# Attention and a gated feed-forward on one core: another order for pairs 0 to 17, and fp32 products of zeros ahead of the first transposes

## The chip, the core and the metric

The kernel runs on one core of a Trainium2 chip. The metric is device time in microseconds (us) for one execution; the time before is the median of three, 401.28 us (401.22 to 402.11). PE is the matrix engine (PEld its weight loads), DVE is VectorE, ACT is ScalarE, POOL is GpSimd, and SP is the engine whose queue issues most transfers.

## The reference

Cosine attention over 8 batches of 12 heads, 448 positions, 64 columns each, and behind it a feed-forward with a hard-swish gate:

```
q_n = q / (norm(q) + 1e-6);  k_n = k / (norm(k) + 1e-6)
scores = q_n @ k_n.T / tau;  attn = softmax(scores);  x = attn @ v
h = x @ w_in;  g = h * clip(h + 3, 0, 6) / 6;  out = g @ w_out
```

x has 3584 rows (8 x 448) of 768 columns, w_in is 768 x 2048, w_out 2048 x 768. All inputs and the output are fp32; the kernel multiplies in bf16.

## The kernel before, in words

Heads are worked on in pairs. There are 48 pairs (six to a batch). The first 18 pairs are run by a list written out by hand, PLAN (lines 21 to 63), one token for each step; from pair 18 (FIRST) on a loop (lines 1017 to 1073) does the same steps in a fixed order. A token only says in which order a step's instructions stand on the engines that it uses; every engine executes its own instructions in order, and waits on the other engines where data or a buffer requires it. So two tokens that use different engines may stand either way round without a difference, and two on one engine may not.

Items are the loads of q and k: items 2d and 2d + 1 are q and k (or the other way round from item 14 on) of pairs 2d and 2d + 1. The tokens that the change touches most, with the first number the item or the pair:

- LQ.j loads item j (line 201, SP queue) into one of seven buffers, which LQ.j can only reuse when the item seven before it has been normalised. LV.d loads v for two pairs, four issues on SP (line 216). W is the next piece of the weights (line 926), issued on POOL.
- SQ.j.e.c.n squares n of the seven column groups (128 columns each) of item j, from group c on, on engine e: a is ACT (line 227), p is POOL, v is DVE (line 229). BN and BS get the sums of squares of some groups from moments on DVE (lines 250 to 256), RE reduces the squares to sums on DVE (line 244).
- NO.d.x makes the inverse norm r of one item or both: logarithm and exponential on ACT (lines 280, 281), and again logarithm and exponential on ACT (286, 287) or, with v, a reduction and a reciprocal on DVE (283, 284).
- NM.j.e multiplies an item by its r (line 297), whole or, with a last 0 or 1, one head pair's half of it. TR.j transposes it on PE (line 343, seven products with the identity), CQ and CK copy the transposed queries and keys out of PSUM (lines 363, 365), and CS the rest of the keys.
- SC.i.g makes the scores of pair i in four groups g on PE (lines 443, 446), EX.i.g their exponentials on ACT (line 464, 896 columns, or 448), VC casts v, VA.i.g multiplies the exponentials with v into PV on PE (line 486), FI divides by the sums on DVE (506, 507), BK transposes back on PE (line 520) and CX copies that to xT.
- U is the next unit of the feed-forward (six products of 448 columns, line 596, or eight of 384 columns, line 756), UH a piece of such a unit, UA and UV its ends on ACT (line 613) and DVE (line 619).
- DP.n and D.n are n products of zeros on PE (lines 938, 933), whose output is never read: 97 in all, 49 of them ahead of TR.1.

The scores of pairs 0 to 5 use two banks of PSUM (SC.i.g.bank). OPEN, behind EX.5.3, gives those back, and from pair 6 on scores, transposes and feed-forward units take turns on a ring of six banks. In the list before, a transpose can name its bank (Y or Z).

Of the kernel before, what the change touches and what calls it, by code (L numbers as in the profile page):

```python
# [66 lines left out]
def kernel(
# [209 lines left out]
    def inverse(tiles, pairs, on_vector):
        n2, le, r = tiles
        ln, nr = n2, pairs[:, :, :, 0]
        nc.scalar.activation(out=ln, in_=n2, func=AF.Ln)  # L280
        nc.scalar.activation(out=nr, in_=ln, func=AF.Exp, scale=0.5)
        if on_vector:
            nc.vector.tensor_reduce(out=le, in_=pairs, axis=AX.X, op=ALU.add)
            nc.vector.reciprocal(out=r, in_=le)
        else:
            nc.scalar.activation(out=le, in_=nr, func=AF.Ln, bias=eps_bias)
            nc.scalar.activation(out=r, in_=le, func=AF.Exp, scale=-1.0)  # L287

    def normalise(j, e, *heads):
# [7 lines left out]
        engines[e].tensor_tensor(  # L297
            out=nrm[:, :, g, :].rearrange("p c g d -> p g c d"),
            in0=raw_of[j][:, g, :, :],
            in1=n2_and_r[2][:, d % 2, j % 2, :]  # L300
            .rearrange("p (g c) -> p g c", g=2)[:, g, :]
            .to_broadcast([128, n, 7, D]),
# [631 lines left out]

    def busy_pv(n):
        first = ("VA", 0, 0) not in issued
        for _ in range(n):
            nc.tensor.matmul(  # L938
                PV[:, 0, 260:508], zeros[:, 0:128], zeros[:, 0:248], start=first, stop=first, skip_group_check=True
            )  # L940

# [174 lines left out]
```

## Time and profile before

| | us |
|---|---|
| median of three runs | 401.28 |
| the profiled execution, its time | 400.82 |
| its span, first to last instruction | 398.9 |
| first products of the feed-forward (line 596) start | 40.28 |
| first products of the second layer (line 756) start | 93.49 |

The profile is of one execution. A line of a timeline gives start, length, engine, source line, operation, output and input, shape and count, and in brackets how long the engine sat idle before it and what ended that. A chain of waits is followed back from the last instruction, at each step to what released it. Windows give the busy time of each engine in a stretch. A matmul's length has its latency in it, so products that follow each other overlap in the table, and a full PE need not be at its peak.

### The profile page before, as it was taken

What the parts mean: (1) busy time and instruction counts of PE and PEld (TensorE: products, weight loads), DVE (VectorE), ACT (ScalarE), POOL (GpSimd) and SP (SyncE); (2) the same over time, 40 slices, a digit from 0 to 9 for tenths busy, and PEclk for the clock granted to TensorE, in tenths of its full rate; (3) what the DMA queues carried; (4) which work ended last, traced back from release to release, by engine and by line L of the source; (5) the groups of instructions that cost most, each with busy time, mean ns of one, the idle gap of its engine ahead of it and who ended that gap; (6) DMA issues with size and microseconds to landing.
All of it is one profiled execution on the core that took longest, in us unless ns stands there. A gap on an engine that the chain in (4) does not pass through costs nothing.

```text
span 398.9 us, 9651 instructions
## 1 busy us (share of the span) xinstructions
PE 390.8 (98%) x3688; PEld 232.1 (58%) x3689; DVE 294.1 (74%) x537; ACT 276.9 (69%) x600; POOL 234.4 (59%) x234
## 2 busy tenths in 40 slices
PE   8899999999999999999999999999999999999996
PEld 6566555555555556555565556565565556555554
DVE  7998898999687787677767786686756565645663
ACT  5999889895678677777868769678658755235230
POOL 6999628662566987488468757858656400400070
PEclk9999999999999999999999999999999999999999
DMA  8999989998869569784889577985863423130134
GB/s 289 314 226 231 221 182 264 204 213 191 202 128 235 123 161 172 181 217 113 196 207 212 130 130 183 190 183 125 194 152 68 99 46 69 41 79 20 31 71 99
DMA packets 93166, 63.75 MB, mean 160 GB/s; under 512 B 56128, under 2 KB 93120, under 8 KB 93120
## 3 DMA queue, kind: packets, MB, share of 16 engines
q1 hardware_dynamic: 87408, 56.45, 60.7%
q0 software_dynamic: 5312, 6.29, 9.3%
q8 instruction: 29, 0.48, 0.5%
q10 hardware_dynamic: 400, 0.39, 0.3%
q14 instruction: 17, 0.14, 0.1%
HBM read 45.61 MB, written 11.01 MB: 142 GB/s over the span
## 4 chain that ended last, share of the span: by engine, by line
PE 92%; ACT 3%; DVE 2%; DMA 1%; issue 1%; POOL 0%; SPq 0%; DVEq 0%
PE M L596 25%; PE M L756 17%; PE PV L486 11%; PE Z L596 6%; PE Y L756 6%; PE M L446 5%; PE Y L596 5%; PE Z L756 5%; PE M L836 3%; ACT at L464 2%; PE Y L446 1%; PE Z L446 1%; PE Z L836 1%; PE PV L938 1%; DMA big<-in_q_dram 1%; PE SC L446 1%
## 5 line engine op out<-in xcount | busy, mean ns | idle before, releaser
L596 PE MATMUL M<-xT,w_in_sb 128*128 128x448 bf16 x540 | 114.6, 353 | 0.0
L464 ACT ACTIVATE at<-M 128x448 bf16<-128x448 f32 x195 | 96.9, 567 | 20.0 <-PE M L446 10.2
L596 PEld LDWEIGHTS <-w_in_sb 128*128 128x128 bf16 x768 | 72.2, 98 | 64.1 <-issue 3.8
L229 POOL TENSOR_TENSOR big<-big 128x896 f32<-128x896 f32 (+5 forms) x47 | 69.5, 1481 | 21.4 <-DMA big<-in_k_dram 10.5
L297 POOL TENSOR_TENSOR nrm<-big,r 128x896 bf16<-128x896 f32 (+1 forms) x45 | 75.7, 1685 | 8.1 <-ACT r L287 5.7
L619 DVE SCALAR_TENSOR_TENSOR gT<-u,M 128x448 bf16<-128x448 bf16 x80 | 49.0, 618 | 34.1 <-ACT u L613 33.5
L613 ACT ACTIVATE u<-M,bias 128x448 bf16<-128x448 f32 x90 | 58.1, 653 | 22.3 <-PE M L596 21.6
L486 PEld LDWEIGHTS <-at 128*128 128x128 bf16 (+1 forms) x1536 | 53.8, 97 | 20.5 <-issue 10.6
L486 PE MATMUL PV<-vx,at 128*128 128x65 bf16 (+1 forms) x1536 | 62.2, 193 | 0.1
L244 DVE TENSOR_REDUCE n<-big 128x14 f32<-128x896 f32 (+1 forms) x48 | 51.1, 1068 | 2.5 <-POOL big L229 2.5
L785 POOL TENSOR_TENSOR big<-big 128x384 f32<-128x384 f32 x12 | 12.8, 1066 | 59.0 <-ACT big L804 59.0
L403 POOL COPY km<-tT 64x128 bf16<-64x128 bf16 x34 | 12.5, 368 | 56.8 <-DMA tT<-nrm 25.9
L756 PEld LDWEIGHTS <-gT 128*128 128x128 bf16 x320 | 30.9, 98 | 21.4
L507 DVE TENSOR_TENSOR on<-PV,rc 128x512 bf16<-128x512 f32 x48 | 33.2, 692 | 1.7
L756 PEld LDWEIGHTS <-gs 128*128 128x128 bf16 x248 | 23.9, 98 | 16.0 <-issue 0.2
L464 ACT ACTIVATE at<-Y 128x448 bf16<-128x448 f32 x51 | 28.9, 566 | 6.1 <-PE Z L446 5.6
L756 PE MATMUL M<-w_out_sb,gT 128*128 128x384 bf16 x176 | 32.2, 326 | 0.0
L446 PE MATMUL M<-tT,kz 64*128 64x448 bf16 (+1 forms) x175 | 31.6, 351 | 0.3 <-ACT at L464 0.3
L464 ACT ACTIVATE at<-Z 128x448 bf16<-128x448 f32 x48 | 27.1, 564 | 3.2 <-PE Z L446 2.2
L756 PE MATMUL M<-w_sum,gs 128*128 128x384 bf16 (+1 forms) x168 | 29.1, 318 | 0.0
L596 PE MATMUL Z<-xT,w_in_sb 128*128 128x448 bf16 x132 | 28.6, 352 | 0.0
L731 DVE TENSOR_TENSOR gs<-gT 128x1024 bf16<-128x1024 bf16 x30 | 26.5, 884 | 0.0
(133 smaller groups left out, 563.3 us busy)
## 6 DMA issues: line engine op xcount, KB each, us to landing
big<-in_k_dram SPq DMA_DIRECT2D x24, 448.0 KB, 4.6
big<-in_q_dram SPq DMA_DIRECT2D x24, 448.0 KB, 4.4
out_dram<-o SPq DMA_DIRECT2D x107, 96.0 KB, 2.2
big<-in_v_dram SPq DMA_DIRECT2D x48, 128.0 KB, 4.2
big<-in_v_dram SPq DMA_DIRECT2D x48, 96.0 KB, 4.3
w_in_sb<-in_moe_w_in_dram POOLq DMA_DIRECT2D x8, 384.0 KB, 7.9
w_out_sb<-in_moe_w_out_dram POOLq DMA_DIRECT2D x4, 768.0 KB, 11.7
tT<-nrm SPq DMA_TRANSPOSE x34, 2.9
```

The costliest lines, as they stand in the source:

```text
L229: engines[e].tensor_tensor(out=o, in0=i, in1=i, op=ALU.mult)
L244: nc.vector.tensor_reduce(out=sums_of(j, c0, n), in_=sq[:, :, c0 : c0 + n, :], axis=AX.X, op=ALU.add)
L297: engines[e].tensor_tensor(out=nrm[:, :, g, :].rearrange("p c g d -> p g c d"), in0=raw_of[j][:, g, :, :], in1=n2_and_r[2][:, d % 2, j % 2, :]
L446: nc.tensor.matmul(o, ks, qt[rows], start=True, stop=True)
L464: nc.scalar.activation(out=o, in_=x, func=AF.Exp, scale=inv_tau)
L486: nc.tensor.matmul(pv_out(j, h), at[rows, n, q_cols(i // HP, j)], vt[rows, 3 + h if name == "M" else 5 * h + int(name[1]), :], start=(name ...
L507: nc.vector.tensor_tensor(out=on[:, :, :, :].rearrange("p j h d -> p h j d"), in0=pv4[:, :, :, 0:D], in1=rc[:, :, :].to_broadcast([128, 2, ...
L596: nc.tensor.matmul(ps[:, 0:S], w_in_sb[:, cc, fc * 128 : (fc + 1) * 128], xT[b % 2][:, cc, 0:S], start=(cc == 0), stop=(cc == CC - 1), ski ...
L613: nc.scalar.activation(out=u[:, :], in_=ps[:, 0:S], func=AF.Relu, bias=half_bias, scale=1.0 / 6.0)
L619: nc.vector.scalar_tensor_tensor(out=g[:, fc, c0 : c0 + S], in0=u[:, :], scalar=1.0, in1=ps[:, 0:S], op0=ALU.min, op1=ALU.mult,)
L731: nc.vector.tensor_tensor(out=o[:, :, :], in0=x, in1=y, op=op)
L756: nc.tensor.matmul(m, lhs[:, c, :], rhs[:, c, c0 : c0 + width], start=(base is None and c == 0), stop=(c == KC - 1), skip_group_check=True,)
```

## The change

The list PLAN is written anew for pairs 0 to 17; the steps, and the loop from pair 18, are the same. What differs beside the order:

- the sharing of squares between engines: SQ.1 wholly on ACT (512 columns: 128 and 384), SQ.0 640 columns on ACT and 256 on POOL (before 512 and 384), SQ.5 wholly on ACT (768 and 128), SQ.7 512 on ACT and 384 on POOL (before 384 and 512), SQ.12 on ACT and SQ.13 on DVE instead of POOL
- NM.1 half on POOL and half on DVE instead of both on DVE; NM.2 both halves on POOL; NM.11 half on DVE and half on POOL
- NO is two steps, NA (the first logarithm and exponential) and NV (the rest), so that other instructions can stand between them
- the first CK.0 on DVE, CQ.11 on ACT
- every transpose, score and unit takes its bank from a written string, RING
- DQ.n, n products of zeros in fp32, whose operands are the same zeros read as fp32; 15 DQ and 9 DP are left of the 97 products of zeros, 11 DQ and 3 DP of these ahead of TR.1
- in SP's queue LQ.8 stands behind the four issues of LV.1 (before: ahead of them) and LQ.11 behind LV.2; the first twelve issues are the same
- VA.4.2 and VA.4.3 stand ahead of SC.6.0 on PE.

```diff
 PLAN = [
-    "LQ.1 BN.1.0.3 DP.3 DP.5 DP.1 DP.1 DP.1 DP.1 DP.2 DP.1 DP.2 DP.6 DP.2 DP.2 DP.1 DP.1 DP.2 DP.1 DP.1 DP.1",
-    "SQ.1.p.3.2 SQ.1.a.5.2 DP.1 DP.2 DP.3 BS.1.0.3 DP.1 DP.4 LQ.0 DP.2 RE.1.3.4 SQ.0.p.0.3 DP.1 DP.1 LQ.3",
-    "SQ.3.p.0.4 SQ.0.a.3.4 RE.0 LQ.2 NO.0.1 NM.1.v.0 NM.1.v.1 SQ.3.a.4.3 NO.0.0 NM.0.p.1",
-    "SQ.2.a.4.3 TR.1.Z NM.0.p.0 LQ.5 SQ.2.a.0.4 D.1 DP.1 RE.3 CK.0.a SQ.5.p.0.4 SQ.5.a.4.3 RE.2 NO.1.v TR.0.Y LQ.4",
-    "CQ.0.a SQ.4.p.4.3 DP.2 SQ.4.a.0.4 DP.3 NM.3.p DP.1 RE.5 CQ.1.v RE.4 LV.0 SC.0.0.0 LQ.6 DP.3 VC.0.v NM.2.v.1",
-    "EX.0.0 SC.0.1.1 NM.2.p.0 CK.1.v LQ.7 LQ.8 DP.5 EX.0.1 SC.0.2.0 EX.0.2 DP.1 VC.1.v DP.1 DP.1 SC.0.3.1 EX.0.3 DP.2",
-    "VA.0.0 DP.2 LV.1 SQ.6.p.0.7 VA.0.1 SC.1.0.0 NO.2.v NM.4.v.1 SC.1.1.1 TR.2.Y DP.1 NM.4.p.0 SQ.7.a.4.3 DP.1 RE.6",
-    "DP.1 DP.1 EX.1.0 EX.1.1 SC.1.2.0 TR.3.Z EX.1.2 CK.2.v DP.1 CQ.2.v SQ.7.p.0.4 DP.1 DP.1 VA.0.2 VA.0.3 SQ.8.a.4.3",
...
-    "CK.6.v EX.5.1 VC.6.p VC.7.p EX.5.2 SC.5.3.1 CK.7.v VA.4.0 EX.5.3 VA.4.1 OPEN CS.7.v SC.6.0 EX.6.0 VA.4.2",
-    "VA.4.3.t CS.6.v FI.4 SC.6.1 EX.6.1 SC.6.2 SC.6.3 EX.6.2 TR.8 CQ.8.v BK.3 VA.5.0 CX.3.v W SQ.12.p.0.7 CQ.9.v",
...
+    "LQ.1 SQ.1.a.3.1 BN.1.0.3 BS.1.0.3 LQ.0 SQ.1.a.4.3 RE.1.3.4 SQ.0.a.2.5 NA.0.1 LQ.3 SQ.3.a.4.3 NV.0.1 SQ.0.p.0.2",
+    "LQ.2 SQ.3.p.0.4 NM.1.p.1 RE.0.0.7 NA.0.0 SQ.2.a.0.4 LQ.5 NV.0.0 NM.1.v.0 NM.0.p.0 RE.3 DQ.11 DP.3 TR.1",
+    "SQ.2.a.4.3 RE.2.0.7 SQ.5.a.1.6 SQ.5.a.0.1 LQ.4 CK.0.v LV.0 NA.1 NM.0.p.1 DQ.2 DP.1 TR.0 SQ.4.p.4.3 CQ.0.a",
+    "SQ.4.a.0.4 NV.1.v RE.5 NM.3.p CQ.1.v DQ.1 SC.0.0.0 LQ.6 EX.0.0 VC.0.v RE.4.0.7 NM.2.p.0 SC.0.1.1 EX.0.1 DQ.1",
+    "DP.1 SC.0.2.0 DP.2 SC.0.3.1 EX.0.2 NM.2.p.1 EX.0.3 LQ.7 CK.1.v NA.2 DP.2 SC.1.0.0 VC.1.v NV.2.v EX.1.0 VA.0.0",
+    "VA.0.1 SQ.6.p.0.7 LV.1 SC.1.1.1 NM.4.v.1 TR.2 CQ.2.v RE.6.0.7 EX.1.1 NM.4.p.0 SQ.7.a.3.4 SC.1.2.0 EX.1.2",
+    "SQ.7.p.0.3 TR.3 LQ.8 SC.1.3.1 NM.5.p CK.2.v VC.3.p LQ.10 LQ.9 VA.0.2 VA.0.3 LV.2 FI.0 RE.7 LQ.11 SQ.8.a.0.4",
+    "SC.2.0.0 SQ.8.a.4.3 CK.3.v VA.1.0 EX.1.3 EX.2.0 SC.2.1.1 NA.3 RE.8 VA.1.1 EX.2.1 SC.2.2.0 EX.2.2 SQ.9.p.4.3 LV.3",
...
+    "VA.4.0 EX.5.2 LQ.15 EX.5.3 OPEN CK.6.v W VC.7.p VA.4.1 CS.6.v CX.1.v VA.4.2 VA.4.3.t SC.6.0 EX.6.0 SC.6.1 EX.6.1",
...
+    "EX.7.2 CS.9.v EX.7.3 VA.6.3.t SC.8.0 FI.6 BK.5 UH.0.0 UH.0.1 UH.0.2 EX.8.0 CX.5.v VA.7.0 U SQ.13.v.0.7 VA.7.1 UA",
+    "VA.7.2 VA.7.3.t SQ.12.a.0.7 SC.8.1 EX.8.1 UV RE.12.0.3 RE.12.3.4 W SC.8.2 UH.1.0 UH.2.0 UH.2.1 EX.8.2 RE.13.0.7",
...
+RING = "233223232234501234501234...
...
-    ring = []
+    ring = [None, None, Y, Z, None, None]
...
-    def busy(n):
-        bank_of("Y", 0)
-        for _ in range(n):
-            nc.tensor.matmul(Y[:, :], zeros[:, 0:128], zeros[:, :], start=True, stop=True)
-
-    def busy_pv(n):
+    def busy_pv(n, z=None):
+        z = zeros if z is None else z
         first = ("VA", 0, 0) not in issued
         for _ in range(n):
             nc.tensor.matmul(
-                PV[:, 0, 260:508], zeros[:, 0:128], zeros[:, 0:248], start=first, stop=first, skip_group_check=True
+                PV[:, 0, 260:508], z[:, 0:128], z[:, 0:248], start=first, stop=first, skip_group_check=True
             )
+
+    def busy_fp32(n):
+        busy_pv(n, zeros.bitcast(FP32))
```

More of the change, by code (lines that the diff above doesn't have):

```diff
@@ L159 @@
     Z = psum.tile([128, 512], FP32, name="Z", tag="Z")
-    ring = []
+    ring = [None, None, Y, Z, None, None]
     ring_n = [0]
     def next_bank():
+        n = ring_n[0]
         ring_n[0] += 1
-        return ring[(ring_n[0] - 1) % len(ring)]
+        return ring[int(RING[n]) if n < len(RING) else (n - len(RING) + int(RING[-1]) + 1) % len(ring)]
     raw_of, sq_of, nrm_of, at_of, on_of = {}, {}, {}, {}, {}
-    engines = {"v": nc.vector, "p": nc.gpsimd, "a": nc.scalar, "s": nc.sync}
+    engines = {"v": nc.vector, "w": nc.vector, "p": nc.gpsimd, "a": nc.scalar, "s": nc.sync}
     issued = set()
@@ L256, in sums_of_moments, with norm_tiles, inverses, in_psum @@
         nc.vector.scalar_tensor_tensor(out=sums_of(j, c0, n), in0=mean, scalar=1.0, in1=m2, op0=ALU.mult, op1=ALU.add)
+    def norm_tiles(d, items):
+        items = tuple(x for x in items if x != "v") or (0, 1)
+        it = slice(items[0], items[-1] + 1)
+        return items, [t[:, d % 2, it, :] for t in n2_and_r], nr_eps[:, d % 2, it, :, :]
     def norms(d, *items):
-        on_vector, items = "v" in items, tuple(x for x in items if x != "v")
+        norms_root(d, *items)
+        norms_inverse(d, *items)
+    def inverses(j, g):
+        n = j // 2 % 2 * 2 + j % 2
+        c = slice(7 * g, 7 * g + 7)
+        if any(x in PLANNED for x in (f"NM.{j}.w", f"NM.{j}.w.{g}")):
+            return PV[:, 1, 264 + 14 * n : 278 + 14 * n][:, c]
+        return n2_and_r[2][:, j // 2 % 2, j % 2, c]
+    def in_psum(j):
+        return [any(x in PLANNED for x in (f"NM.{j}.w", f"NM.{j}.w.{g}")) for g in range(2)]
+    def norms_root(d, *items):
         needs(("NM", 2 * d - 4), ("NM", 2 * d - 3))
-        items = items or (0, 1)
+        items, tiles, pairs = norm_tiles(d, items)
         for x in items:
             needs(("RE", 2 * d + x))
-        it = slice(items[0], items[-1] + 1)
-        inverse([t[:, d % 2, it, :] for t in n2_and_r], nr_eps[:, d % 2, it, :, :], on_vector)
+        root(tiles, pairs)
+    def norms_inverse(d, *args):
+        items, tiles, pairs = norm_tiles(d, args)
+        le, r = tiles[1:]
+        parts = [(le, r)]
+        if any(any(in_psum(2 * d + x)) for x in items):
+            parts = []
+            for n, x in enumerate(items):
+                h = in_psum(2 * d + x)
+                n7 = PV[:, 1, 264 + 14 * (d % 2 * 2 + x) : 278 + 14 * (d % 2 * 2 + x)]
+                if h[0] == h[1]:
+                    parts.append((le[:, n, :], n7 if h[0] else r[:, n, :]))
+                else:
+                    for g in (0, 1) if h[0] else (1, 0):
+                        c = slice(7 * g, 7 * g + 7)
+                        parts.append((le[:, n, c], n7[:, c] if h[g] else r[:, n, c]))
+        inverse(tiles, pairs, "v" in args, parts)
         for x in items:
@@ L272, in norms_two, with root @@
         needs(*(("NM", 2 * d + x) for x in range(-4, 0)), *(("RE", 2 * d + x) for x in range(4)))
+        assert not any(any(in_psum(2 * d + x)) for x in range(4))
         two = [t.rearrange("p e i c -> p (e i) c") for t in n2_and_r]
-        inverse(two, nr_eps.rearrange("p e i c x -> p (e i) c x"), on_vector)
+        pairs = nr_eps.rearrange("p e i c x -> p (e i) c x")
+        root(two, pairs)
+        inverse(two, pairs, on_vector)
         issued.update(("NO", x, y) for x in (d, d + 1) for y in range(2))
-    def inverse(tiles, pairs, on_vector):
+    def root(tiles, pairs):
         n2, le, r = tiles
@@ L281, in inverse @@
         nc.scalar.activation(out=nr, in_=ln, func=AF.Exp, scale=0.5)
+    def inverse(tiles, pairs, on_vector, parts=None):
+        n2, le, r = tiles
+        nr = pairs[:, :, :, 0]
+        parts = parts or [(le, r)]
         if on_vector:
             nc.vector.tensor_reduce(out=le, in_=pairs, axis=AX.X, op=ALU.add)
-            nc.vector.reciprocal(out=r, in_=le)
         else:
             nc.scalar.activation(out=le, in_=nr, func=AF.Ln, bias=eps_bias)
-            nc.scalar.activation(out=r, in_=le, func=AF.Exp, scale=-1.0)
+        for x, o in parts:
+            if on_vector:
+                nc.vector.reciprocal(out=o, in_=x)
+            else:
+                nc.scalar.activation(out=o, in_=x, func=AF.Exp, scale=-1.0)
     def normalise(j, e, *heads):
@@ L296, in normalise @@
         n = len(heads)
+        assert e == "w" or not any(in_psum(j)[x] for x in heads)
+        if n == 1 or e == "w":
+            r = inverses(j, heads[0]) if n == 1 else PV[:, 1, 264 + 14 * (j % 4) : 278 + 14 * (j % 4)]
+        else:
+            r = n2_and_r[2][:, d % 2, j % 2, :]
         engines[e].tensor_tensor(
@@ L321, in bank_of @@
     def bank_of(name, reads):
-        bank = {"Y": Y, "Z": Z}[name] if name else next_bank()
+        bank = next_bank()
         key = id(bank)
```

14 lines of the change are left out of this document (7 added, 7 removed), and 59 rows, old and new, of the table PLAN.

## The prediction

> **What bounds the kernel now.** I read the busy line of the page first, then busy time in five stretches, then the chain of waits of the first 48 us, and last the groups of ScalarE by shape in the stretch where the chain lies on it.
>
> ```profile
> PE 390.8 (98%) x3688; PEld 232.1 (58%) x3689; DVE 294.1 (74%) x537; ACT 276.9 (69%) x600; POOL 234.4 (59%) x234
> 0.00:12.40 12.40, 9.79 (x73) 7.45 (x75) 9.10 (x37) 7.78 (x20) 9.22 (x24) 1.00 0.89 285
> 12.40:34.10 21.70, 20.63 (x283) 13.31 (x283) 21.12 (x49) 21.32 (x38) 21.66 (x19) 1.00 1.01 273
> 34.10:43.00 8.90, 8.72 (x165) 6.15 (x164) 6.49 (x22) 7.88 (x18) 8.88 (x11) 1.00 1.12 208
> 43.00:93.40 50.40, 50.28 (x499) 27.82 (x498) 47.56 (x90) 45.72 (x99) 27.89 (x27) 1.00 1.06 211
> 93.40:398.90 305.50, 301.41 (x2677) 177.38 (x2673) 209.78 (x343) 194.16 (x428) 166.81 (x156) 1.00 0.61 137
> ```
>
> The columns of a stretch are its length, then busy time of PE, PEld, DVE, ACT and POOL, the granted clock and the DMA share. From 43.0 us on PE is the only full engine (50.28 of 50.40, then 301.41 of 305.50), and the work there is the same in both kernels. What the change can win is therefore how much sooner PE reaches that state. From 12.4 to 34.1 us all four engines are nearly full (20.63, 21.12, 21.32 and 21.66 of 21.70): nothing is gained there by moving work from one to another, only by removing idle time or work.
>
> ```profile
> 10.77 0.56 PE Y L343 x7
> 11.33 0.64 PE PV L938 x6
> 12.00 0.36 PE SC L446 x2
> ...
> 30.86 3.29 ACT at L464 x5
> 34.16 0.04 issue
> 34.20 0.36 PE M L446 x2
> 34.56 0.58 PE PV L486 x15
> ...
> 37.16 0.11 PE PV L938
> ```
>
> The chain runs through PE early, with the products of zeros (L938) on it, and hands over to ScalarE's exponentials (L464): the first scores of pair 6 (34.20) wait for the last exponential of pair 5, because OPEN gives the score banks to the ring only then. So 34.16 us, the end of EX.5.3, is the date to be moved. ScalarE's groups between 12.35 and 34.16 us:
>
> ```profile
> L464 ACT ACTIVATE at<-SC 128x896 bf16<-128x896 f32 x18 | 15.5, 918 | 0.1
> L464 ACT ACTIVATE at<-SC 128x448 bf16<-128x448 f32 x6 | 3.3, 542 | 0.2
> L281 ACT ACTIVATE nr<-n 128x28 f32<-128x28 f32 x4 | 0.9, 229 | 0.1
> ```
>
> All its idle time there is 0.1 + 0.2 + 0.1 = 0.4 us (21.70 less 21.32 says the same). EX.5.3 ends at the start of EX.0.0 plus ScalarE's work plus that 0.4.
>
> **The products ahead of the first transposes.** 49 bf16 products become 11 fp32 and 3 bf16; of the other 48 products of zeros only 4 fp32 and 6 bf16 stay.
>
> ```profile
> 1.06 7.36 PE L938 MATMUL PV<-xT 128*128 128x248 bf16 x49 [1.06 <-DVE xT L983]
> 1.06 7.09 PEld L938 LDWEIGHTS <-xT 128*128 128x128 bf16 x49 [1.06 <-DVE xT L983]
> 1.00:3.00 2.00, 1.94 (x10) 1.44 (x11) 1.00 0.50 90
> 5.00:7.00 2.00, 2.00 (x20) 1.81 (x19) 1.00 1.05 392
> 9.08 0.56 PE L343 MATMUL Z<-ident,nrm 128*128 128x128 bf16 x7 [0.66 <-DVE nrm L297]
> ```
>
> Two windows of L938 alone hold 10 products at first and 20 later, so PE begins at half pace (about 0.2 us each) and doubles near 5 us, though the granted clock reads 1.00 in both; at full pace it is 0.64 / 6 = 0.107 us each (11.33). No row shows an fp32 product. The lower bound is one bf16 product each: 11 x 0.2 = 2.2 us, ending at 3.3. The upper bound is four, each with its weight load in the open: 4 x (0.2 + 0.145) = 1.38 us at first (7.09 / 49 = 0.145), three of them to 5.2 us, then eight at 4 x (0.107 + 0.1) = 0.83, ending near 12. I take four with the load hidden, since in the 49 the load is hidden already (7.09 inside 7.36) and each operand is twice as wide in bytes, which makes four products of halves: 0.8 us five times to 5.2, six at 0.43, ending at 7.8, and 8.1 with the three bf16. That is ahead of the transposes at 9.08 and costs nothing; if the cover goes, each us past 9.1 is a us on the first transposes. The Trainium skill, "FP8 and Floating Point Precision", section TensorE Precision Notes, states that true FP32 makes 4 passes through the array; no run here shows it yet, and by it the end would be the 7.8 us that I take. "TensorE: Matmul & The Clock Gate", section on weight-path perf modes, of the same skill speaks against the change: the fast weight load is off for FP32, and the sum would lie toward the 12 us.
>
> **The first pairs.** This is where the new order costs.
>
> ```profile
> 5.45 0.63 ACT L227 ACTIVATE big<-big 128x512 f32<-128x512 f32 x1 [0.77 <-DMA big<-in_q_dram]
> 6.00 0.22 ACT L280 ACTIVATE n<-n 128x14 f32<-128x14 f32 x1
> 6.50 0.31 ACT L286 ACTIVATE le<-nr,bias 128x14 f32<-128x14 f32 x1
> 6.83 0.21 ACT L287 ACTIVATE r<-le 128x14 f32<-128x14 f32 x1
> 6.96 1.04 POOL L229 TENSOR_TENSOR big<-big 128x512 f32<-128x512 f32 x1 [0.64 <-DMA big<-in_k_dram]
> 7.36 1.66 DVE L297 TENSOR_TENSOR nrm<-big,r 128x448 bf16<-128x448 f32 x2
> 8.31 0.21 ACT L287 ACTIVATE r<-le 128x14 f32<-128x14 f32 x1
> 8.60 2.11 POOL L297 TENSOR_TENSOR nrm<-big,r 128x448 bf16<-128x448 f32 x2 [0.60 <-ACT r L287]
> 11.85 0.63 ACT L227 ACTIVATE big<-big 128x512 f32<-128x512 f32 x1
> 12.40 3.01 ACT L464 ACTIVATE at<-SC 128x896 bf16<-128x896 f32 x4
> ```
>
> Item 0's square on ScalarE grows from 512 to 640 columns: 0.63 x 128/512 bounds it at 0.16, I take 0.1. The norm of item 1 is now cut in two, with SQ.3.a between the halves. That square needs the load of item 3, which lands at 6.96 (POOL's wait). So the second half starts at about 7.5 where it started at 6.50, and r of item 1 is there at about 7.95 where it was at 6.83 + 0.21 = 7.04: 0.9 late. It is nearly paid back, because NM.1 is split: one half on VectorE (0.83) and one on POOL (2.11 / 2 = 1.05, behind SQ.3.p that ends at 8.0) beside each other, ending at 9.05, where two in a row on VectorE ended at 9.02. TR.1 stays at 9.1. Item 0 is not paid back: its norm follows on ScalarE with a 512 square inside (0.55, from 11.85 to 12.40), so r of item 0 is ready at 7.95 + 0.45 + 0.55 + 0.55 = 9.5 at most, 9.3 with starts overlapping, where it was 8.52. NM.0 on POOL takes 1.9 to 2.11 more, to 11.2 to 11.6 instead of 10.71. TR.0, CQ.0, SC.0.0 and EX.0.0 hang on it one behind the other: EX.0.0 starts 0.5 to 0.9 late. I take 0.7.
>
> **From there to pair 6.** ScalarE's work after EX.0.0 gets 128 more columns of squares (SQ.7: 512 instead of 384), 0.1 us. The larger share of items 1 and 5 lies ahead of EX.0.0 and is in the 0.7. The 0.4 of idle time goes, since PE runs ahead of ScalarE without the products of zeros, 46 of them between 9 and 34 us:
>
> ```profile
> L938 PE MATMUL PV<-xT 128*128 128x248 bf16 x46 | 7.7, 271 | 0.1
> ```
>
> They took 46 x 0.107 = 4.9 us of PE, nearly all in time in which PE would else wait for ScalarE, so they are worth the 0.4 (between 0 and 0.8, if start spacing hides as much again) and not 4.9. What is added to POOL (halves of NM.1 and NM.2, 2 x 1.05) equals the squares that leave it (items 1, 0, 5 and 7: 256 + 128 + 512 + 128 columns, at 1.04 per 512 about 2.1): nothing.
>
> **At pair 6 and after.** VA.4.2 and VA.4.3 now stand ahead of SC.6.0 on PE, in its wait for EX.5.3: the 0.58 us at 34.56 leaves the path. The product of zeros at 37.16 goes: 0.11. Then SQ.12 and one copy of CQ.11 move to ScalarE and SQ.13 to VectorE.
>
> ```profile
> 41.00:60.00 19.00, 18.93 (x206) 10.68 (x204) 16.93 (x34) 16.66 (x36) 7.74 (x7) 1.00 1.00 201
> ```
>
> 896 columns are 1.1 us at 0.63 per 512, the copy 0.4: 1.5 into ScalarE's 2.3 us of slack there (19.00 less 16.66). I cost it at nothing; without that slack it is up to 1.5. The weight transfers stay between POOL operations and land well ahead of their readers: nothing. The loop from pair 18 is the same.
>
> **Sum.** +0.7 (EX.0.0 late) + 0.1 - 0.4 - 0.58 - 0.11 = -0.3 us. The profiled execution took 400.8 us (span 398.9 and 1.9 around it), the median is 401.3; less 0.3 that is 401.0. By the bounds, +0.9 + 0.1 - 0 - 0.7 = +0.3 and +0.5 + 0.1 - 0.8 - 0.7 = -0.9.
>
> **The rivals.** (a) Faster by more: PE's 50.28 of 50.40 busy hides waits, since a product of 6 x 0.19 us counts as busy while it waits for its bank, and the new order of units, exponentials and copies from pair 8 on closes some. For it: VectorE is at 47.56 of 50.40 there, so small orders matter. Against it: ScalarE and VectorE get more work just there. Beside the lower bound of -0.9 it would bring a further 0.7 to 1.7: 398.7 to 399.7. (b) Slower by a load: ScalarE executes in order, and SQ.8.a stands ahead of EX.1.3.
>
> ```profile
> 11.21 0.42 SPq L201 DMA_DIRECT2D big<-in_q_dram  x1
> 14.35 0.53 SPq L201 DMA_DIRECT2D big<-in_q_dram  x1
> big<-in_q_dram SPq DMA_DIRECT2D x1, 448.0 KB, 5.0
> big<-in_q_dram SPq DMA_DIRECT2D x1, 448.0 KB, 5.9
> ```
>
> The load of item 8 is issued at 11.21 and lands 5.0 later. In the new order it stands behind the four issues of LV.1, where the load of item 10 stood (14.35, 5.9 to land), and LQ.7 ahead of both waits for NM.0, which is 0.5 to 0.9 late. In that place it lands at 20.3 to 21.2; one load fewer ahead of it speaks for 19. ScalarE comes to SQ.8.a at about 19.3: 13.1, four exponentials (2.9), half a norm (0.44), three exponentials at 0.8 and a square (0.55). From a landing of 20.8 on the sum is over +1.2: 402.5 to 403.1. (c) Slower by the clock: without the products PE drops to the half pace of 1 to 5 us somewhere between 9 and 34. PE's busy time there without them is about 20.6 - 4.5 = 16.1, partly latency; at half pace 22 to 32 us against 21.7, so some 4 us longer: 405. Against it: the transposes at 10.77 ran in the same 0.56 as those at 9.08, after idle times like the 0.66 us shown there. The Trainium skill, "TensorE: Matmul & The Clock Gate", section on the clock gate, lets the clock fall only after an idle window of about 3.4 us, which this order doesn't have; by that rule the time stays 401. (d) The fp32 products end near 12 us: TR.1 comes 2.9 late and EX.0.0 some 2, 402.5 to 403.
>
> **How the numbers follow.** About 0.3% (1.2 us) is what a measurement of this kernel can tell from no change. Forecast within that 0.39, (a) 0.31, (b) 0.14, (c) 0.08, (d) 0.08. Some 0.03 of (b) and (d) together ends inside 0.3%, so faster 0.31, same 0.42, slower 0.27. Point 401.0; the forecast's own range 400.1 to 402.2; with the others to eight in ten 398.7 to 403.4.
>
> **What would show it.** Right: the first products end at 8.1 us, TR.1 starts near 9.1 and TR.0 near 11.5; EX.0.0 starts at 13.1; ScalarE has no idle time to EX.5.3, which ends near 34.4; VA.4.3 stands ahead of SC.6.0; PE is full from there. Wrong: ScalarE idle ahead of SQ.8.a by a DMA (b), products of 448 columns 0.37 us apart after 12 us (c), L343 later than 9.5 behind L938 (d), or a loop from pair 18 that begins more than 1.2 us earlier than before (a).

## The result, and the profile after

The changed kernel takes 404.17 us in the median of 20 runs (401.89 to 407.77), the kernel before 401.74 us on the same chip (20 runs): a ratio of 1.0050 with a 95% interval of 1.0028 to 1.0071. It is slower by 2 us, outside the predicted range of 398.7 to 403.4. The profiled execution took 403.70 us, its span is 401.9 us, and the one of before 398.9: 3.0 us to explain.

For the sizes below one thing has to be known: each run lists its mean granted TensorE clock, and executions under 0.997 are some 2 us longer than the others of the same kernel (56 of the 128 executions of before in the later comparisons, 11 of the 20 of the changed kernel), so one profile alone doesn't settle a difference of 1 us, and the last column of the table of experiments takes the other executions alone.

The stretches of the prediction once more, after the change (length, then busy time of PE, PEld, DVE, ACT and POOL, the clock, DMA):

```profile
12.40:34.10 21.70, 18.67 (x263) 11.88 (x261) 20.00 (x44) 21.46 (x38) 20.69 (x18) 1.00 1.05 259
34.10:43.00 8.90, 8.02 (x150) 5.58 (x150) 7.93 (x25) 7.67 (x18) 7.17 (x11) 1.00 1.14 222
43.00:93.40 50.40, 50.40 (x504) 27.95 (x505) 46.84 (x89) 47.07 (x102) 28.25 (x26) 1.00 1.01 206
93.40:105.00 11.60, 9.31 (x91) 5.38 (x90) 9.34 (x15) 5.76 (x13) 5.47 (x5) 1.00 1.03 225
```

Up to 34 us ScalarE is as full as before (21.46 against 21.32), PE has 2 us less to do without the zeros, and from 43 to 93 us PE is full. The last line is the one that differs: PE has 9.31 of 11.60 us, where in the profile of before it is busy for all 11.60. PE there, start and length in the first two columns, the idle time before it in brackets, in the changed kernel and then in the one before:

```profile
98.14 1.46 PE L806 MATMUL M<-w_out_sb,gT 128*128 128x384 bf16 x8
99.54 0.29 PE L536 MATMUL PV<-vx,at 64*128 64x65 bf16 x8
102.12 0.54 PE L496 MATMUL M<-tT,kz 64*128 64x448 bf16 x3 [2.29 <-DMA tT<-nrm]
102.61 1.47 PE L806 MATMUL Z<-w_sum,gs 128*128 128x384 bf16 x8
```

```profile
97.88 1.46 PE L756 MATMUL Z<-w_out_sb,gT 128*128 128x384 bf16 x8
99.28 0.55 PE L446 MATMUL M<-tT,kz 64*128 64x448 bf16 x4
99.88 1.47 PE L756 MATMUL Y<-w_sum,gs 128*128 128x384 bf16 x8
```

(Lines of the changed kernel are 49 or 50 higher: 806 is 756, 496 is 446.) The last of three equal units starts 0.26 us later than before (98.14 and 97.88), the next product group 2.73 us later (102.61 and 99.88). Between them stands SC.16.0, the first scores of pair 16, for which PE sits idle 2.29 us: it reads what XD.17 brings, a DMA that transposes item 17 (XD does by a transfer what TR does on PE; XP does it for results). What the DMA waited for is in SP's queue (start, length of the issue), before and after:

```profile
92.88 1.28 SPq L544 DMA_TRANSPOSE xT<-on  x1
94.27 1.23 SPq L354 DMA_TRANSPOSE tT<-nrm  x1
95.55 0.58 SPq L201 DMA_DIRECT2D big<-in_k_dram  x1
96.20 2.58 SPq L216 DMA_DIRECT2D big<-in_v_dram  x4
98.90 1.27 SPq L354 DMA_TRANSPOSE tT<-nrm  x1
```

```profile
92.48 1.28 SPq L594 DMA_TRANSPOSE xT<-on  x1
93.80 0.60 SPq L203 DMA_DIRECT2D big<-in_q_dram  x1
94.45 2.59 SPq L218 DMA_DIRECT2D big<-in_v_dram  x4
97.16 2.19 SPq L404 DMA_TRANSPOSE tT<-nrm  x1
99.39 0.58 SPq L203 DMA_DIRECT2D big<-in_k_dram  x1
```

Before, XD.17 is issued at 94.27, directly behind XP.12 (L544). In the new list LQ.23 (L203) and the four issues of LV.9 (L218) stand between them, 3.2 us of issues, and XD.17 is issued at 97.16. It lands 4.8 us later, where in the profile of before it landed 3.1 us after its issue. The chain of waits of the changed kernel runs through it:

```profile
97.04 0.11 ACT big L854
97.16 4.83 DMA tT<-nrm
```

The list of what differs tells SP's order only to LQ.11; this second place is in the new list as well ("XP.12 UA LQ.23 UV SC.15.1 LV.9 ... XD.17"), and neither list nor prediction looked there. Of the 3.0 us of span, 2.73 are there at 102.61; the last 0.3 come behind it and were not followed.

### The profile page after: what moved, and what is told of

The parts are those of the page before. It is cut to its first block, busy times and chain, and to the rows that moved or that the text cites. A ratio compares the mean times of both kernels' runs of the same rounds, so it can differ in the third digit from the quotient of the medians.

```text
span 401.9 us, 9537 instructions
## 1 busy us (share of the span) xinstructions
PE 389.5 (97%) x3631; PEld 230.6 (57%) x3631; DVE 294.4 (73%) x536; ACT 278.3 (69%) x603; POOL 232.9 (58%) x233
## 4 chain that ended last, share of the span: by engine, by line
PE 89%; ACT 4%; DMA 2%; DVE 2%; POOL 1%; issue 0%; SPq 0%; POOLq 0%; DVEq 0%
PE M L646 25%; PE M L806 17%; PE PV L536 11%; PE Z L646 6%; PE M L496 6%; PE Z L806 6%; PE Y L646 5%; PE Y L806 4%; PE M L886 3%; ACT at L514 3%; PE Z L496 1%; PE Y L496 1%; PE Y L886 1%; DMA big<-in_k_dram 1%; DMA tT<-nrm 1%; POOL nrm L349 1%
## 5 line engine op out<-in xcount | busy, mean ns | idle before, releaser
L646 PE MATMUL M<-xT,w_in_sb 128*128 128x448 bf16 x528 | 111.7, 352 | 0.0
L349 POOL TENSOR_TENSOR nrm<-big,r 128x896 bf16<-128x896 f32 (+1 forms) x48 | 78.1, 1633 | 7.3 <-ACT r L334 5.0
L231 POOL TENSOR_TENSOR big<-big 128x896 f32<-128x896 f32 (+5 forms) x43 | 63.6, 1481 | 26.0 <-DVE n L246 9.2
L669 DVE SCALAR_TENSOR_TENSOR gT<-u,M 128x448 bf16<-128x448 bf16 x77 | 47.5, 619 | 36.7 <-ACT u L663 36.4
L246 DVE TENSOR_REDUCE n<-big 128x14 f32<-128x896 f32 (+2 forms) x49 | 51.3, 1050 | 1.5 <-POOL big L231 0.8
L453 POOL COPY km<-tT 64x128 bf16<-64x128 bf16 x34 | 13.9, 409 | 58.2 <-PE M L496 21.7
L806 PEld LDWEIGHTS <-gT 128*128 128x128 bf16 x320 | 30.8, 98 | 21.6 <-DVE gT L781 0.4
L806 PE MATMUL M<-w_out_sb,gT 128*128 128x384 bf16 x200 | 36.4, 326 | 0.0
L806 PEld LDWEIGHTS <-gs 128*128 128x128 bf16 x248 | 23.8, 98 | 16.6 <-DVE gs L781 0.4
L496 PE MATMUL M<-tT,kz 64*128 64x448 bf16 x174 | 31.1, 351 | 2.3 <-DMA tT<-nrm 2.3
L806 PE MATMUL M<-w_sum,gs 128*128 128x384 bf16 (+1 forms) x168 | 29.9, 322 | 0.0
L646 PE MATMUL Z<-xT,w_in_sb 128*128 128x448 bf16 x126 | 27.3, 353 | 0.0
L366 POOL CAST vx<-big 128x512 bf16<-128x512 f32 x38 | 26.3, 692 | 0.1
```

Of the source, the lines that this page charges most:

```text
L231: engines[e].tensor_tensor(out=o, in0=i, in1=i, op=ALU.mult)
L246: nc.vector.tensor_reduce(out=sums_of(j, c0, n), in_=sq[:, :, c0 : c0 + n, :], axis=AX.X, op=ALU.add)
L349: engines[e].tensor_tensor(out=nrm[:, :, g, :].rearrange("p c g d -> p g c d"), in0=raw_of[j][:, g, :, :], in1=r.rearrange("p (g c) -> p g ...
L366: (engines[e].copy if e == "a" else engines[e].tensor_copy)(out=o, in_=f)
L496: nc.tensor.matmul(o, ks, qt[rows], start=True, stop=True)
L646: nc.tensor.matmul(ps[:, 0:S], w_in_sb[:, cc, fc * 128 : (fc + 1) * 128], xT[b % 2][:, cc, 0:S], start=(cc == 0), stop=(cc == CC - 1), ski ...
```

## The experiments

Every kernel was run in five rounds beside the kernel before. In the diffs only the tokens that move are shown. The last column has the number of executions with a mean clock of 0.997 or more, and their median less that of before's in the same comparison (for the change, less 401.06, the median of all 72 such executions of before).

| kernel | median, us | ratio to before, 95% interval | clock 0.997 or more: count, us |
|---|---|---|---|
| the change (20 runs) | 404.17 | 1.0050 (1.0028 to 1.0071) | 9, +2.3 |
| xd17_first | 404.06 | 1.0037 (1.0009 to 1.0066) | 7, +1.8 |
| lv9_behind | 403.17 | 1.0036 (1.0012 to 1.0060) | 10, +1.8 |
| before_sp_order | 402.24 | 1.0025 (1.0000 to 1.0049) | 8, +0.9 |
| before_few_zeros | 400.77 | 0.9972 (0.9948 to 0.9995) | 12, -0.3 |
| start_only | 402.33 | 0.9998 (0.9969 to 1.0028) | 8, +0.3 |
| rest_only | 403.80 | 1.0048 (1.0015 to 1.0080) | 8, +2.1 |
| cut_at_9 | 401.88 | 0.9996 (0.9969 to 1.0024) | 8, +0.5 |
| cut_at_13 | 401.42 | 1.0000 (0.9973 to 1.0028) | 10, 0.0 |
| tail_before_sp_after | 404.43 | 1.0059 (1.0038 to 1.0080) | 3, +1.9 |
| copy_first | 403.46 | 1.0049 (1.0023 to 1.0075) | 7, +2.0 |
| both_first | 401.99 | 1.0012 (0.9985 to 1.0039) | 8, +0.8 |
| start_tail_before | 401.90 | 0.9992 (0.9965 to 1.0018) | 9, +0.2 |
| after_filled | 404.79 | 1.0065 (1.0037 to 1.0094) | 9, +3.1 |
| tail_filled | 404.00 | 1.0051 (1.0016 to 1.0085) | 5, +2.0 |

The kernel before, run anew in each of the four comparisons, had medians of 401.62, 401.92, 401.34 and 402.16 us, so ratios are compared, not medians. The ratios are no quotients of the medians: for xd17_first that quotient is 1.0061, for tail_before_sp_after 1.0077. Differences of 0.1 to 0.2% between two kernels are therefore not told apart here.

### The place of XD.17 alone

The changed kernel with XD.17 ahead of the five issues:

```diff
-XP.12 UA LQ.23 UV SC.15.1 LV.9 ... XD.17 FI.14
+XP.12 XD.17 UA LQ.23 UV SC.15.1 LV.9 ... FI.14
```

> The changed kernel with one token moved: XD.17 (the transposing transfer of item 17, whose result the scores of pair 16 read) stands directly behind XP.12 in SP's queue, ahead of LQ.23 and of the four issues of LV.9, as it did before the change; nothing else on any engine moves. Theory (the transfer is issued 2.9 us late, at 97.16 instead of 94.27 us, and SC.16.0 waits 2.29 us for it): XD.17 is issued near 93.8, lands near 97, PE has no wait ahead of SC.16.0, and the time falls by 2.0 to 2.5 us, to within 0.5 us of the kernel before. Rival 1 (the wait only uncovers another one behind it, such as DVE's or ScalarE's work of pair 15): the wait at SC.16.0 is less, but most of the 2.3 us comes back within 20 us; the time falls by less than 1 us. Rival 2 (the time is lost by the new start, pairs 0 to 7): no change of the time.

The kernel before with the changed order of those issues:

```diff
-UA LQ.23 VA.13.1 ... XP.12 SC.15.0 ... XD.17 LQ.22 LV.9
+UA VA.13.1 ... XP.12 LQ.23 LV.9 SC.15.0 ... XD.17 LQ.22
```

> The kernel before with the changed kernel's SP order at this place alone: LQ.23 and LV.9 stand between XP.12 and XD.17 (LQ.23 stood ahead of LV.10, LV.9 behind LQ.22). Theory: XD.17 is issued near 97.2 instead of 94.27 us, lands near 102, SC.16.0 waits some 2.3 to 2.6 us, and the time is 2.0 to 2.6 us longer than before (ratio 1.005 to 1.0065). Rival 1: the wait is there, but the time grows by less than 1 us, since PE catches up. Rival 2 (loss in the start): no change.

And the change with LV.9 alone behind XD.17 (LQ.23 stays ahead):

```diff
-XP.12 UA LQ.23 UV SC.15.1 LV.9 ... XD.17 FI.14
+XP.12 UA LQ.23 UV SC.15.1 ... XD.17 LV.9 FI.14
```

> The changed kernel with LV.9's four issues behind XD.17, but LQ.23 still ahead of it; nothing else moves. Theory (it is the count of issues ahead of XD.17 on SP, 0.65 us each, against a slack of some 1.9 us that the kernel before had at SC.16.0): XD.17 is issued near 94.5, lands at 97.7 to 99.3, the wait at SC.16.0 is 0 to 0.3 us, and the time falls by 1.8 to 2.5 us. Rival (the 448 KB of LQ.23, which now lie ahead of the transposing transfer in the DMA engines, hold it up as they did): it lands after 101, a wait of 1.5 us or more stays, and the time falls by less than 1 us.

In xd17_first no wait for the DMA is left. In lv9_behind there is one of 0.5 us and in before_sp_order a new one of 0.8 us, each one row of PE's waits:

```profile
PE M L496 <- DMA tT<-nrm: 0.5, 1, 0.5
PE M L446 <- DMA tT<-nrm: 0.8, 1, 0.8
```

So the mechanism is there, but the times did not follow: taking the wait away left 1.0037 of 1.0050. Something else holds as much. In before_sp_order the wait is smaller than expected because XD.17, behind the same five issues, landed 3.4 us after its issue and not 4.8. Over the profiles of all kernels here its landing takes 3.4 to 5.2 us behind the five issues, 2.8 to 5.3 us ahead of them, and 5.8 us in lv9_behind. What the place costs is therefore the 2.9 us of later issue. That it makes the landing longer is not shown, and the 3.1 us of before is among the short ones.

### Which stretch carries the loss

Four hybrids, all with the few zeros of the change. start_only takes the new order up to OPEN and the old one behind it, rest_only the reverse (five tokens that only one of the lists has ahead of OPEN follow it, or are left out of the new rest); cut_at_9 and cut_at_13 go over to the old order behind FI.9 and FI.13.

```diff
 start_only:  new list to OPEN,  old list from CS.7.v on
 rest_only:   old list to OPEN,  new list from CS.6.v on
 cut_at_9:    new list to FI.9,  old list from LQ.16 on
 cut_at_13:   new list to FI.13, old list from LQ.23 on
```

> The changed order up to the opening of the ring (pairs 0 to 5), and from there on the order of before; the few zero products of the change throughout. Theory A (the loss sits behind pair 9, where XD.17 stands behind LQ.23 and LV.9): as before_few_zeros, 400.5 to 401.2 us. Theory B (part of the loss is the changed start: the first product of MM1 at 40.97 us in place of 40.28): 401.3 to 402.5 us.

> The order of before up to the opening of the ring, with the few zero products, and the changed order from there on. Theory A: the wait of SC.16.0 for XD.17 is there and the time is 401.7 to 403.2 us, that is 1 to 2.3 us over before_few_zeros. Theory B: some 1 us over before_few_zeros, and the rest of the loss shows in start_only.

> The changed order through the output of pair 9, from there on the order of before (XD.17 ahead of nothing but what stood ahead of it before). Theory A: no wait for XD.17, 400.5 to 401.2 us. Theory B: the loss of start_only stays and what pairs 6 to 9 add comes on top: 401.5 to 402.8 us.

> The changed order through the output of pair 13, from there on the order of before; LQ.23 comes directly behind LV.8 again, LV.9 behind XD.17. Theory A: no wait for XD.17, 400.5 to 401.2 us. Theory B: as cut_at_9, and a difference to it belongs to pairs 10 to 13; 401.5 to 402.8 us.

The three that end in the old order are at 1.000; rest_only, with the old start, has the whole loss (1.0048, more than theory A's 401.7 to 403.2 us), and its profile the wait of 2.3 us again. The medians of start_only and cut_at_9 (402.33 and 401.88) lie in theory B's ranges, but theirs was the comparison in which before had 401.92, and the last column has +0.3 and +0.5. Theory A holds as to the place: within the 0.3% of the intervals nothing is lost ahead of FI.13, and the loss is in pairs 14 to 17. The same four profiles show how far one execution can be trusted: cut_at_9 and cut_at_13 are the same list up to pair 9, and their first product of line 756 (802 there) starts 1.16 us apart.

The zeros by themselves, in the kernel before (its 49 products ahead of TR.1 become 11 fp32 and 3 bf16 ones, the other 48 become 4 and 6):

```diff
-DP.3 DP.5 DP.1 ... TR.1.Z ... D.1 DP.1 ... DP.2 ... DP.5
+DQ.11 DP.3 TR.1.Z ... DQ.2 DP.1 ... DQ.1 ... DQ.1 DP.1
```

> The kernel before with the products of zeros of the changed one and nothing else: 11 fp32 and 3 bf16 ahead of the first transposes instead of 49 bf16, and 4 fp32 and 6 bf16 instead of 48 after them, at the same scores. Forecast's step (they lie in PE's waiting time, worth the 0.4 us that ScalarE idles between EX.0.0 and EX.5.3): 0 to 0.8 us faster, ScalarE's last exponential of pair 5 ends 0.3 to 0.8 us sooner than 34.15. Rival (PE loses its full pace without them): products of 448 columns stand 0.37 us apart after 12 us, and the time is 2 us or more longer. Rival (the fp32 products end later than 9.1 us): TR.1 later than 9.2.

0.9972 (0.9948 to 0.9995) is the only ratio here whose interval lies below 1. But none of its 12 executions ran under 0.997, where 15 of the 35 of before beside it did, and in the last column the gain is 0.3 us. The other kernels with the few zeros have 2 to 9 such executions of 12, so the few zeros do not prevent them, and most of the microsecond may be chance. The step itself does not show in the one profile: between the start of EX.0.0 and the end of EX.5.3 lie 21.72 us (before 21.75), and EX.5.3 ends at 34.73, where 0.3 to 0.8 us sooner than 34.15 was expected. TR.1 is later than the 9.2 us named, yet not for the fp32 products, which had ended 1.19 us earlier:

```profile
9.38 0.56 PE L341 MATMUL Z<-ident,nrm 128*128 128x128 bf16 x7 [1.19 <-DVE nrm L295]
```

With the new start (start_only, cut_at_9) the ratio is 1.000; the intervals overlap, so a cost of the new start of up to a microsecond is neither shown nor excluded.

### Two losses in line

The profile of xd17_first, an execution that is 2 to 3 us late from its start on, has a wait of 0.66 us for DVE behind the place of the one for XD.17. PE, DVE and POOL of that execution:

```profile
105.27 1.46 PE L806 MATMUL Z<-w_sum,gs 128*128 128x384 bf16 x8 [0.66 <-DVE big L863]
```

```profile
102.89 1.86 DVE L631 COPY gT<-gT 128x1024 bf16<-128x1024 bf16 x1
104.67 0.54 DVE L863 TENSOR_TENSOR big<-Z,big 128x384 f32<-128x384 f32 x1
```

```profile
102.78 1.68 POOL L349 TENSOR_TENSOR nrm<-big,r 128x896 bf16<-128x896 f32 x1
```

and of the kernel before:

```profile
98.97 0.42 DVE L581 COPY gT<-gT 128x1024 bf16<-128x1024 bf16 x1
```

```profile
98.70 1.54 POOL L786 TENSOR_TENSOR big<-big,o 128x384 f32<-128x384 f32 x1 [0.31 <-ACT o L775]
100.76 1.69 POOL L297 TENSOR_TENSOR nrm<-big,r 128x896 bf16<-128x896 f32 x1
```

The copy is GL.0, the left columns of the gate. In the new list it comes behind pair 15's division (FI.15) and so meets NM.19, the normalisation on POOL: 1.86 us in place of 0.42. It ends at 104.75, the drain of a unit (L863) behind it is late, and the product that needs the bank waits. In the changed kernel itself the copy takes 1.86 us too, but PE stands still for XD.17 in that time, so its profile names only the one wait. That gives a two by two: XD.17 forward, GL.0 forward, both.

```diff
 copy_first, both_first:
-GS.1 U UA UA VA.15.3.t UP FI.15 SC.16.0 VC.16.p GL.0 NM.19.p
+GS.1 GL.0 U UA UA VA.15.3.t UP FI.15 SC.16.0 VC.16.p NM.19.p
 both_first also:
-XP.12 UA LQ.23 UV SC.15.1 LV.9 ... XD.17
+XP.12 XD.17 UA LQ.23 UV SC.15.1 LV.9 ...
```

> The changed kernel with GL.0 alone ahead of the reciprocal of pair 15. Theory C: the copy is 0.4 to 0.5 us, but the wait of SC.16.0 for XD.17 is still 1.5 to 2.5 us and hides the gain: 403.3 to 404.5 us. Rival (the copy is the main loss, not XD.17): 401.5 to 402.5 us.

> The changed kernel with two undone: XD.17 directly behind XP.12 (as in xd17_first), and VectorE's copy of the left columns (GL.0) ahead of the reciprocal of pair 15, as before. Theory C (two losses in line, the one hidden by the other: the wait for XD.17, and the copy of 1.86 us in place of 0.42 that meets GpSimd's normalisation of item 19 and holds the drain for which the product L806 waits): no DMA wait, a copy of 0.4 to 0.5 us, no wait L806 <- DVE, and 400.6 to 401.8 us, against 404.1 with XD.17 alone. Rival (the loss is the order of pairs 14 to 17 on TensorE): 403 to 404 us as with XD.17 alone.

Neither alone pays much (1.0037 and 1.0049 against 1.0050), both together give 1.0012. In the profile of both_first there is no wait for the DMA and none of L806 for DVE:

```profile
99.46 0.29 PE L536 MATMUL PV<-vx,at 64*128 64x65 bf16 x8
99.59 0.54 PE L496 MATMUL M<-tT,kz 64*128 64x448 bf16 x3
100.06 1.47 PE L806 MATMUL Z<-w_sum,gs 128*128 128x384 bf16 x8
```

The size expected for the copy was wrong: it took 1.22 us there, not 0.4 to 0.5, over another operation of POOL, but nothing waited for it:

```profile
99.08 1.22 DVE L631 COPY gT<-gT 128x1024 bf16<-128x1024 bf16 x1
```

```profile
98.88 1.14 POOL L836 TENSOR_TENSOR big<-big,o 128x384 f32<-128x384 f32 x1 [0.30 <-ACT o L825]
```

The interval of both_first (0.9985 to 1.0039) overlaps those of the change, of xd17_first and of copy_first, so that the two losses stand in line is likely and not shown clear of the noise. In the last column both together bring 1.5 of the 2.3 us, and each alone 0.5 and 0.3. What remains there, 0.8 us, was not traced; with the whole old tail (cut_at_13) it is 0.0.

The rest of the tail was tried from the other side: cut_at_13 with the changed place of LQ.23 and LV.9 and nothing else, and the change for pairs 6 to 13 alone.

```diff
 tail_before_sp_after:
-FI.13 LQ.23 EX.14.1 ... XP.12 SC.15.0 ... XD.17 LQ.22 LV.9
+FI.13 EX.14.1 ... XP.12 LQ.23 LV.9 SC.15.0 ... XD.17 LQ.22
 start_tail_before:
 old list to OPEN, new list to FI.13, old list from LQ.23 on
```

> As cut_at_13, with LQ.23 and LV.9 between XP.12 and XD.17 as the change has them. Theory C: a wait for XD.17 of 0.5 to 1 us, as in before_sp_order, and 0.5 to 1 us over cut_at_13: 401.8 to 402.6 us; the copy stays 0.42 us. Rival (the order on SP alone carries the loss): 403 us and more.

> The order of before through pair 5 and from pair 14 on, the changed order for pairs 6 to 13 alone, with the few zero products. Theory C: nothing of the loss lies in it; as before_few_zeros or up to 0.5 us less (the profile of rest_only was 0.3 to 0.5 us ahead of before at 95 us): 400.0 to 401.0 us. Rival (pairs 6 to 13 cost too): 401.5 us and more.

tail_before_sp_after missed theory C's size: 1.0059 against 1.0000 for cut_at_13, intervals apart, where 0.5 to 1 us was expected. Two tokens on SP's queue, five issues, cost 0.6%, the whole loss: this is the clearest of the experiments. The copy missed too, with 1.22 us where 0.42 was expected, but nothing waited for it. The profiled execution of tail_before_sp_after had its whole start 2.5 us late and a wait of 1.1 us; tail_filled (below), with the same order and a start in time, shows what the wait is otherwise. Pairs 6 to 13 in the new order cost nothing that shows (0.9992), though the median of 401.90 us lies in the rival's range.

### A price behind the wait

copy_first's profile holds more than the wait. PE, and PE's clock (the number ahead of the last two in a row) in stretches of 1 us:

```profile
102.03 0.79 PE L496 MATMUL M<-tT,kz 64*128 64x448 bf16 x3 [2.20 <-DMA tT<-nrm]
102.79 2.74 PE L806 MATMUL Z<-w_sum,gs 128*128 128x384 bf16 x8
```

```profile
102.00:103.00 1.00, 0.97 (x5) 0.27 (x6) 0.00 (x0) 0.52 (x2) 1.00 (x2) 0.59 1.04 321
103.00:104.00 1.00, 1.00 (x4) 0.46 (x3) 0.00 (x0) 1.00 (x4) 0.59 (x1) 0.50 1.27 185
104.00:105.00 1.00, 1.00 (x4) 0.46 (x3) 0.00 (x0) 0.34 (x1) 0.00 (x0) 0.50 1.08 351
105.00:106.00 1.00, 1.00 (x11) 0.31 (x10) 0.36 (x1) 0.10 (x1) 0.00 (x0) 0.71 0.69 111
```

After 2.20 us without work the granted clock is at half for about 3 us, and eight products take 2.74 us in place of 1.47: 1.27 us on top of the wait. The changed kernel's own profile, with 2.29 us of idle time, has no such stretch. The Trainium skill, "TensorE: Matmul & The Clock Gate", part on the HAM clock gate, gives the drop after an idle window of about 3.4 us that runs freely; here it came after 2.2, and the measurement decides. The four rows lack 1.7 us of full clock, 0.4% of the execution, and its mean clock is 0.995. To see whether this wait is behind most of the executions' lower clock, the wait was filled with 30 products of the identity ahead of SC.16.0, in two kernels.

```diff
 after_filled, tail_filled:
-SC.16.0
+DI.30 SC.16.0
 DI.n: n products  PV[:, 0, 260:388] <- ident, ident   (never read)
```

> The changed kernel with 30 products of the identity by itself (128 columns) directly ahead of SC.16.0, where TensorE waits for XD.17; nothing reads them. Theory D (a wait of 2.2 us and more costs its own length and, in part of the executions, a stretch at half clock behind it, as in the profile of copy_first): the 2.3 us stay, as 1.6 to 1.8 us of products and a wait of under 1 us; fewer executions have a granted clock under 0.997 (11 of 20 in the changed kernel), and the median falls by 0.5 to 1.3 us, to 402.9 to 403.7 us. Rival (the lower clock comes from the start alone): about the changed kernel's 404.2 us, and the same share.

> tail_before_sp_after with the same 30 products ahead of SC.16.0. Theory D: fewer executions under 0.997 than its 9 of 12, and 402 to 403.2 us against 404.4. Rival: 404 us and more, and as many.

It is not. tail_filled has 7 of 12 executions under 0.997 (9 of 12 without the fill) and 1.0051; after_filled has 3 of 12, but no gain in time (1.0065), since its fill starts 1.0 us late, behind DVE's division. Theory D is not supported as the main cost. The other two profiles with a mean clock under 0.997 show another place: in xd17_first (0.995) and tail_before_sp_after (0.996) the half clock lies near 12 to 15 us and costs the same 1.7 us. In xd17_first, ScalarE, PE and the clock:

```profile
8.71 0.52 ACT L229 ACTIVATE big<-big 128x384 f32<-128x384 f32 x1 [2.18 <-DMA big<-in_k_dram]
11.20 0.56 PE L393 MATMUL Y<-ident,nrm 128*128 128x128 bf16 x7 [2.68 <-POOL nrm L349]
14.00:15.00 1.00, 1.00 (x5) 0.38 (x6) 1.00 (x2) 0.94 (x2) 1.00 (x2) 0.50 0.76 155
```

The load of item 3 lands late, SQ.3.a waits 2.18 us for it (1.17 in tail_before_sp_after), everything behind it comes late, PE has nothing to do for 2.68 us (2.32) ahead of TR.1, and EX.5.3 ends 2.5 us later than in the changed kernel's profile. No profile shows the old start in this state. Their share is the same with either start, 56 of 140 executions with the new one and 67 of 176 with the old, so it hardly bears on the loss; why a load is late in some executions stays open. What tail_filled does show is the length of the wait:

```profile
99.09 1.84 PE L989 MATMUL PV<-ident 128*128 128x128 bf16 x30
101.84 0.54 PE L492 MATMUL M<-tT,kz 64*128 64x448 bf16 x3 [0.91 <-DMA tT<-nrm]
```

PE reaches the fill ahead of SC.16.0 at 99.09, and SC.16.0 starts at 101.84: 2.75 us in an execution whose start was in time, and enough for the 0.6%. In the changed kernel the idle time is 2.29.

## Why the prediction was wrong, point by point

**The step that failed** is the end of the part on pair 6 and after: "The weight transfers stay between POOL operations and land well ahead of their readers: nothing. The loop from pair 18 is the same." No run speaks against either sentence, but between them pairs 7 to 17 were costed at nothing without their queues being walked. Behind that stands the premise of the first part, that all the change can win from 43 us on is "how much sooner PE reaches that state": PE's 50.28 of 50.40 us in the old order was taken to hold for the new one. SP's queue was followed only for the first load that changed place (LQ.8). At XD.17 the new list puts five issues ahead of a transfer that had 1.9 us to spare in the profile of before (issued at 94.27, landed 3.1 us later, read at 99.28). Issued 2.9 us later and landing in 4.8, it is there 2.7 us after that time, and 2.29 of these are idle time of PE. The sum should have had this +2.3 us, about the whole of what was measured. GL.0 moving behind FI.15 was passed over in the same way; its price, 0.66 us in one profile, is not shown clear of the noise.

**The zeros** ahead of TR.1 were right in kind and near in size. The x25 are 11 fp32 products, two records each, and three bf16 ones:

```profile
1.20 7.48 PE L984 MATMUL PV<-xT 128*128 128x248 f32 x25 [1.20 <-DVE xT L1033]
9.26 0.56 PE L393 MATMUL Y<-ident,nrm 128*128 128x128 bf16 x7 [0.58 <-POOL nrm L349]
9.66 1.16 PE L984 MATMUL PV<-xT 128*128 128x248 f32 x5
11.07 0.56 PE L393 MATMUL Z<-ident,nrm 128*128 128x128 bf16 x7 [0.25 <-POOL nrm L349]
```

They end at 8.68 (forecast 8.1), ahead of TR.1 at 9.26 (9.1). At full pace two fp32 products and one bf16 one take 1.16 us with their latency, about half a microsecond for an fp32 one, which fits four passes of 0.107. An end near 12 us (d) did not come. PE did not fall to half pace (c) in this profile or that of before_few_zeros; in those of xd17_first and tail_before_sp_after it did, at 12 to 15 us, but for some 3 us and not for the whole stretch, and whether 49 products would have kept the pace there no run shows. The gain of the zeros, 0.4 (0 to 0.8) and 0.11 in the sum, is 0.3 us in the last column for before_few_zeros and 1.1 (0.2 to 2.1) by its ratio. The rule on weight loads that spoke for 12 us did not decide.

**The first pairs** cost less than forecast in this profile:

```profile
12.66 2.97 ACT L514 ACTIVATE at<-SC 128x896 bf16<-128x896 f32 x4
31.17 2.95 ACT L514 ACTIVATE at<-SC 128x896 bf16<-128x896 f32 x4
```

EX.0.0 starts 0.26 us later than before, not 0.7, because r of item 0 was there at 9.10 and not at 9.3 to 9.5, and EX.5.3 ends at 31.17 + 2.95 = 34.12 (forecast 34.4, before 34.16). From one to the other it is 21.46 us, 0.3 less than before, as summed. Load 8 (rival b) held nobody up. Load 3 did in two other profiles: the forecast took its landing at 6.96 from one execution, and where it came later EX.0.0 started at 15.49 (xd17_first) and 14.79 (tail_before_sp_after).

**At pair 6** the gain of 0.58 + 0.11 us became a loss of 0.69: the first product of the feed-forward starts at 40.97, not 40.28. VA.4.2 and VA.4.3 do run in ScalarE's shadow, but then the ring waits for DVE's copies:

```profile
34.66 0.39 DVE L415 COPY xT<-Z 128x448 bf16<-128x448 bf16 x1
35.19 0.39 DVE L415 COPY kz<-Y 64x64 bf16<-64x64 bf16 x2
```

```profile
35.63 0.35 PE L496 MATMUL Y<-tT,kz 64*128 64x448 bf16 x1 [0.88 <-DVE kz L415]
```

CX.1 (34.66) and CS.7 (35.19) hold banks Z and Y, and the new list has both behind CS.6. By 98 us all but 0.26 of it is made good, and cut_at_13, with the same order there, is at 1.000: this term was mis-sized but does not set the time. SQ.12 and CQ.11 on ScalarE cost nothing that shows, as forecast: ScalarE has 47.07 of 50.40 us, and PE is full.

**The rivals** named four mechanisms, and none was a transfer of the tail; the range's upper end came from the load at the start. The reason given for (a) finds no support: the 540 products of line 596 into bank M take 349 to 364 ns each in the profile of before, so none was recorded longer for waiting.

## What to carry to other kernels

When a list is written anew, compare each engine's order over its whole length, the queue that issues the transfers first: for every transfer that moves behind others, set the time of its issue plus its landing against the time at which it is read, and do so in the stretch where the consuming engine has no slack. Take the time of landing from several profiles, since one may show a short one. When one wait is found and its removal brings little, look in the profile without it for the next wait in line; here two changes that each brought little brought 0.4% together, though the intervals still overlap. And mind what a cheap copy runs beside, since its place decides its length.

## What the runs showed of the hardware

- A copy of 128 x 1024 bf16 on DVE took 0.42 us in some places and 1.86 us beside a normalisation on POOL; where it took 0.42 beside L786, that took 1.54 us, and where it took 1.22 the same POOL operation took 1.14 (over before's execution that operation takes 0.99 to 1.54). So either can be the one that is longer. The Trainium skill, "Advanced Engine Details and Errata", section VectorE Performance Modes, notes that VectorE's second port is shared with GpSimd, and that GpSimd and those VectorE instructions that use both ports block each other; the trace agrees in that both get longer, and which mode the copy ran in no row shows.
- The granted clock went to 0.50 for about 3 us after 2.20 us without work on PE in one profile, and within 1.3 us behind idle times of 2.32 and 2.68 us at the start of two more, and each time 1.7 us of full clock were lost. It stayed at 1.00 after 2.29 us in the changed kernel's profile and after 2.20 us in that of start_tail_before.
- The transposing DMA of XD.17 landed 2.8 to 5.8 us after its issue, by the profile and not clearly by its place: 3.1 in before, 4.8 in the changed kernel, 3.4 in before_sp_order, behind the same five issues as in the changed kernel.
